# First two blocks' triangular inverses by quarters instead of halves, weight loads on another queue, and VectorE's order fixed around the first chain

## The chip, the cores and the metric

One core of one Trainium2 chip. The metric is the device time of one execution in microseconds; the median of three runs is compared. PE is the matmul engine (PEld its weight loads), DVE is VectorE, ACT is ScalarE, POOL is GpSimd, SP is SyncE, which here only issues DMAs.

## The reference

Linear attention with the delta rule, then a two-layer network on its output:

```python
for t in range(S):                       # B=4, H=8, S=768, D=48
    y[:, :, t] = einsum('bhd,bhde->bhe', q[t], state)
    v_old = einsum('bhde,bhd->bhe', state, kt)          # kt: normalized key
    state = state + bt * einsum('bhd,bhe->bhde', kt, vt - v_old)
...
x = attn_out as (3072, 384)
h = x @ w_in                              # w_in 384 x 2048
out = maximum(0.01 * h, h) @ w_out        # w_out 2048 x 384
```

## The kernel before

The 768 steps are cut into 12 blocks of C = 64. In a block, the 32 heads (8 heads of 4 sequences) are independent; they lie in two groups `g` of 16. For each block `n` these stages run:

- `gram(n)`: PE forms, for each head, keys times keys and keys times queries (`pg`). ACT copies the first part to `gs`, which goes out to DRAM (`gd`) and comes back as `L` with one half of one head a partition. DVE masks the second part into `rq`, one ring buffer `q` a group.
- `inv(b)`: DVE computes norms and coefficients (`norms`), scales L and inverts the unit triangular 32x32 halves of each head's 64x64 matrix by elimination (`eliminate`: one step a column, two products and two subtractions). The first call handles blocks 0 and 1 together (`NB[0] = [0, 1]`, all 128 partitions), later calls one block each. The result T goes out to DRAM, also transposed by ACT (`Tt`).
- `merge(n, g, t)`: the halves come back by DMA, into `t` and `gm`; two products on PE (`pz`, `pu`) with copies by ACT and DVE (`zs`, `rt`) give the block that joins the halves.
- `solve(n)`: per group loads of k, v and q (`rk`, `rv`, `rq`), then `pk`, `pw`, `pc` (state) and `py` (output) on PE with ACT copies between them. `rv` is multiplied by the norms on DVE.
- `columns(n)`: PE transposes y; `split` makes a high and a low part of it (`xh` by ACT, `xl` by DVE).
- `ffn(n)`: 16 steps `f`, each nine products to `ph`, the activation by ACT (`gh`), its low part by DVE (`gl`), and six products to `po`.

The two weight matrices come as 32 tiles `w_all[:, k // 2, k % 2]` of 128x384 64-bit words (a double each). `weights()` unpacks tile k into a high and a low float with ACT's `Abs` (L146), seven DVE instructions (L148, L154 to L158, L161) and an ACT cast (L160). `load_w` issues the load, 8 tiles ahead (`WAHEAD`) from tile 14 on; a small DVE memset (L123) in front of the load holds it back to a given place of DVE's order. Only after tile 2f + 1 is unpacked can step f of `ffn(0)` finish. Tiles 0 to 3 are unpacked during the grams, the rest after the first inverse.

The order on each engine is not that of the code: a planner lays all instructions out at build time by priority (order of the trace) and by its own estimate of when inputs are ready. Each engine then runs its list in that order and waits where an input is late. `weave` only sets the order of the trace; `behind(name)` adds the one condition that an instruction comes after the marked one on its engine. DMAs are issued in order from SP's or ACT's queue.

Of the kernel before, what the change touches and what calls it, by code (L numbers as in the profile page):

```python
# [47 lines left out]
def delta_moe_kernel(ctx: ExitStack, tc, kqT, kv, qT, beta, cst, w_all, out, nblk):  # L48
# [31 lines left out]


# [32 lines left out]
    def split(src, hi, lo):  # L114
        nc.scalar.copy(hi, src)
        nc.vector.tensor_tensor(lo, src, hi.bitcast(F32), ALU.subtract)  # L116
# [10 lines left out]
    def weights():  # L127

        for k in range(2 * NFC):
            f, x = k // 2, k % 2
            words = raws.pop(k).bitcast(F32).rearrange("p (n two) -> p two n", two=2)
            lo, hi = words[:, 0], words[:, 1]
            loi, hii = lo.bitcast(U32), hi.bitcast(U32)
            g = sb.tile([P, DO], F32, tag="cg", name=f"cg{k}", bufs=CB)
# [3 lines left out]
            def final():  # L140
                t = sb.tile([P, 2 * DO], F32R, tag=f"w{k}", name=f"w{k}", bufs=1)
                for e in range(2):
                    (wi, wo)[x][e][f] = t[:, e * DO:(e + 1) * DO]
                return (w[f] for w in (wi, wo)[x])

            nc.scalar.activation(g, hi, AF.Abs)  # L146
            with behind("inverse" if k >= KA else None):
                i = nc.vector.tensor_scalar(g, g, HI_MIN, HI_MAX, ALU.max, ALU.min)  # L148
# [8 lines left out]
            nc.vector.scalar_tensor_tensor(ri, loi, 18, ri, ALU.logical_shift_right, ALU.bitwise_or)  # L157
            nc.vector.tensor_scalar(e.bitcast(U32), gi, 0xFF800000, None, ALU.bitwise_and)  # L158
            d0, d1 = final()
            nc.scalar.copy(d0, g)  # L160
# [14 lines left out]
    def gram(n):  # L175
# [11 lines left out]
        if i == 0:  # L187
            Lh[b0] = sb.tile([P, HC, HC], F32, tag="L", name=f"L{b0}", bufs=2)
        gd = dr.tile([64, HC, HC], F32, tag="gd", name=f"gd{n}")
        for g in range(NGR):  # L190
            kq = kqs[g]
            gs = sb.tile([P, 2, NPAIR, C], F32, tag="gs", name=f"gs{n}_{g}", bufs=2)
            gm[n, g] = m = sb.tile([P, 2, GU, HC], F32, tag="gm", name=f"gm{n}_{g}", bufs=GM_BUFS)
# [12 lines left out]
            for c in range(2):  # L206
                for e in range(2):
                    a = e * HS + g * GH + c * GU
                    (nc.sync, nc.scalar)[e if n < 2 else 0].dma_start(
                        gd[a:a + GU].rearrange("l j i -> j l i"),  # L210
                        gs[c * 64 + e * HC:c * 64 + (e + 1) * HC].rearrange("p b u t -> p (b u) t")[:, :, e * HC:(e + 1) * HC])
            qa = of("q", n, g)
            for b in range(2):
                for c in range(2):
                    r = slice(c * 64, (c + 1) * 64)
                    nc.vector.tensor_tensor(  # L216
                        qa[DN, c, b * NPAIR:(b + 1) * NPAIR], pv[b][r, 1],
                        tri[r].rearrange("p (o t) -> p o t", o=1).broadcast_to([C, NPAIR, C]), ALU.mult)
# [12 lines left out]
    def norms(n, n2):  # L231

        p, w = P, HC
        s, r, c, z = (sb.tile([P, wd], F32, tag=t, name=f"{t}{n}", bufs=b)
                      for t, wd, b in (("sr", HC, 1), ("rc", HC, 1), ("cb", HC, 2), ("sq", C, 2)))
        nrm[n] = z
# [11 lines left out]
        nc.vector.tensor_tensor(c, c, r, ALU.mult)  # L248
        for e in range(2):
# [3 lines left out]
    def eliminate(b, L, j, T, m):  # L253


        w = HC - 1 - j
        parts = []
        for x in range(min(m, 2)):
            t = T[:, x:m:2]
            k = t.shape[1]  # L260
            tv = sb.tile([P, 144], F32, tag=f"tmp{x}", name=f"tmp{b}_{j}_{x}", bufs=1)
# [4 lines left out]
            parts.append((tv, t[:, :, j + 1:]))  # L266
        for tv, t in parts:
# [3 lines left out]

    def inv(b):

        for n in NB[b]:
            need(gg, gram, n)
        two = len(NB[b]) > 1
        M = HC if two else HC // 2
# [6 lines left out]
        if two:  # L284
            nc.vector.tensor_copy(X[:, ::HC + 1], c)
        else:
            for e in range(2):
                r = slice(e * 64, e * 64 + 64)
                nc.vector.tensor_copy(X[r, e:M * HC:HC + 2], c[r, e::2])
# [4 lines left out]
        for j in range(HC - 1):  # L294
            eliminate(b, L, j, T, j + 1 if two else j // 2 + 1)
            if j == HC - 2:
                Tt = sb.tile([P, HC * HC], F32, tag="L", name=f"Tt{b}", bufs=2) if two else X[:, M * HC:]
                Tt = Tt.rearrange("p (i m) -> p i m", m=M)
                nc.scalar.copy(Tt.rearrange("p i m -> p m i"), T)
# [12 lines left out]
    def merge(n, g, t):
# [11 lines left out]
        lo, r1 = slice(R0 + HC, P), slice(0, HC)  # L324
        if len(NB[where[n][0]]) == 1:
            r1 = slice(HC, 2 * HC)
            with behind("h"):
                nc.scalar.copy(gt[r1].rearrange("p l (m e) -> p l e m", e=2),
                               gt[0:HC].rearrange("p l (e m) -> p l e m", e=2))
# [24 lines left out]
    def solve(n):  # L354
# [3 lines left out]
        nc.tensor.matmul(ps[DN, 0:HS], nrm[b][i * 64:i * 64 + 64], eye0[i * 64:i * 64 + 64], start=True, stop=True)  # L358
# [3 lines left out]
        def load(g):  # L362
            merge(n, g, of("t", n, g))
# [71 lines left out]
    def columns(n):  # L435
# [4 lines left out]
        for cc in range(NCC):  # L440
# [5 lines left out]
            parts.append((xh, xl))  # L446

# [60 lines left out]
    NS, NF, NI = NSLOT, NFC + 1, HC + 1  # L508
# [28 lines left out]
def _layout(inputs):  # L537
# [20 lines left out]
    bts = np.stack([np.concatenate([bt[0], bt[1]])] + [np.concatenate([bt[n], bt[n]]) for n in range(2, nblk)])  # L558
# [39 lines left out]
```

## Time and profile before

| | us |
|---|---|
| median of 3 runs | 725.72 (724.77 to 726.75) |
| profiled execution: time, span | 727.48, 725.7 |
| busy PE, DVE, ACT, POOL | 627.9, 499.6, 323.8, 7.4 |
| mean granted clock of PE | 0.973 |

Busy time is a sum over the span; a stage can have another limit than the whole. A row of the profile names the line, the engine and the operation, then output and input by the program's names, the shape, the count, the time and what the engine waited for last. Two DVE instructions can overlap by about a tenth of a microsecond in the records, so the time of a sequence is read from starts, not summed from durations.

### The profile page before, as it was taken

To read this page: it belongs to the slowest core of one execution; us is meant where nothing else is said; L and a number is where in the kernel's file an instruction comes from. 1 tells how busy PE (TensorE), PEld (TensorE's weight loads), DVE (VectorE), ACT (ScalarE), POOL (GpSimd) and SP (SyncE) were. 2 spreads that over 40 slices of the span, in tenths; PEclk is the share of its full clock that TensorE was granted. 3 is DMA by queue.
4 is the path that set the end of the run, shared out by engine and by line. 5 is a ranking of instruction groups with operands and counts; after the bars stand their busy time and mean duration, and the time that the engine had idled before them with its cause. 6 is when DMAs were issued, how large, how long until landed. Compare 5 with 4: busy or idle time off the path is not lost.

```text
span 725.7 us, 20966 instructions
## 1 busy us (share of the span) xinstructions
PE 627.9 (87%) x8296; PEld 581.4 (80%) x8296; DVE 499.6 (69%) x2222; ACT 323.8 (45%) x830; POOL 7.4 (1%) x12
## 2 busy tenths in 40 slices
PE   5200789948997999999999999999999999999996
PEld 4100679838986998998989989989989989999996
DVE  7798999999594765866955956947858659532221
ACT  3112656624444463553454444534634635544432
POOL 4000000000000000000000000000000000000000
PEclk9999999967998999999999999999999999999999
DMA  8495783610306427036045064073171260310000
GB/s 196 94 308 106 196 213 91 162 37 23 46 2 121 102 46 162 17 68 153 3 90 131 4 117 105 7 139 77 30 146 48 46 132 2 63 29 2 1 22 23
DMA packets 130786, 60.91 MB, mean 84 GB/s; under 512 B 115392, under 2 KB 118592, under 8 KB 130688
## 3 DMA queue, kind: packets, MB, share of 16 engines
q1 hardware_dynamic: 117376, 56.81, 34.9%
q10 hardware_dynamic: 13312, 2.76, 2.1%
q8 instruction: 65, 1.06, 0.6%
q14 instruction: 33, 0.27, 0.1%
HBM read 46.96 MB, written 12.58 MB: 82 GB/s over the span
## 4 chain that ended last, share of the span: by engine, by line
PE 61%; DVE 22%; DMA 7%; ACT 4%; issue 3%; SPq 2%; ACTq 1%; DVEq 0%
PE ph L468 25%; PE po L458 22%; DMA tt<-T 3%; PE pk L383 3%; DVE rq L216 3%; PE pw L396 3%; DVE rv L388 3%; DVE T L268 2%; DVE tmp L263 2%; PE pu L342 2%; PE pz L334 2%; SPq L307 2%; DVE cg L155 1%; DVE w L161 1%; DVE cr L157 1%
## 5 line engine op out<-in xcount | busy, mean ns | idle before, releaser
L468 PE MATMUL ph<-xh,w 128*128 128x256 f32 x1152 | 257.3, 296 | 10.0 <-DVE gl L475 6.9
L468 PEld LDWEIGHTS ph<-xh,w 128*128 128x128 f32 x1152 | 195.9, 193 | 21.5 <-DVE gl L475 9.7
L458 PE MATMUL po<-w,gh 128*128 128x384 f32 x768 | 192.0, 347 | 8.7 <-ACT w L160 4.9
L475 DVE TENSOR_TENSOR gl<-ph,gh 128x256 fp32r<-128x256 f32 x192 | 80.6, 423 | 134.4 <-ACT ph L473 123.6
L468 PE MATMUL ph<-xl,w 128*128 128x256 f32 x576 | 166.0, 289 | 1.9 <-DVE xl L116 1.1
L472 ACT ACTIVATE gh<-ph 128x256 fp32r<-128x256 f32 x192 | 73.5, 383 | 173.2 <-PE ph L468 170.8
L458 PEld LDWEIGHTS po<-w,gh 128*128 128x128 f32 x768 | 134.1, 193 | 12.1 <-ACT w L160 5.6
L458 PE MATMUL po<-w,gl 128*128 128x384 f32 x384 | 119.7, 345 | 0.0
L468 PEld LDWEIGHTS ph<-xl,w 128*128 128x128 f32 x576 | 111.3, 193 | 4.3 <-DVE xl L116 4.0
L268 DVE TENSOR_TENSOR T<-T,tmp 128x60 f32<-128x60 f32 (+35 forms) x661 | 112.3, 207 | 1.3
L263 DVE TENSOR_TENSOR tmp<-T,L 128x60 f32<-128x60 f32 (+35 forms) x661 | 112.4, 208 | 0.7
L473 ACT ACTIVATE ph<-ph 128x256 f32<-128x256 f32 x192 | 73.1, 381 | 0.0
L458 PEld LDWEIGHTS po<-w,gl 128*128 128x128 f32 x384 | 68.9, 193 | 0.5
L334 PE MATMUL pz<-rt,gm 32*32 32x32 f32 x768 | 19.9, 197 | 34.8 <-DMA rt<-td 34.8
L201 PE MATMUL pg<-kq 48*64 48x128 f32 x768 | 38.5, 301 | 12.5 <-DMA kq<-in_kqT 7.2
L334 PEld LDWEIGHTS pz<-rt,gm 32*32 32x32 f32 x768 | 16.0, 111 | 37.7 <-DMA rt<-td 35.2
L201 PEld LDWEIGHTS pg<-kq 48*64 48x64 f32 x768 | 30.6, 147 | 19.4 <-DMA kq<-in_kqT 8.0
L216 DVE TENSOR_TENSOR rq<-pg,csb 64x256 f32<-64x256 f32 x96 | 40.6, 423 | 1.7
L280 DVE MEMSET T<- 128x512 f32 (+1 forms) x11 | 5.8, 524 | 39.7 <-DMA tt<-T 30.2
L385 ACT ACTIVATE rt<-pk 48x512 f32<-48x512 f32 x44 | 26.1, 593 | 12.6 <-PE pk L383 11.9
L160 ACT CAST w<-cg 128x384 fp32r<-128x384 f32 x32 | 16.1, 510 | 33.6 <-DVE cr L157 24.5
L398 ACT COPY rv<-pw 64x384 f32<-64x384 f32 x48 | 22.7, 472 | 16.1 <-PE pw L396 15.2
(61 smaller groups left out, 651.4 us busy)
## 6 DMA issues: line engine op xcount, KB each, us to landing
wr<-in_w_all SPq DMA_DIRECT2D x32, 384.0 KB, 5.3
kq<-in_kqT SPq DMA_DIRECT2D x44, 192.0 KB, 3.7
L<-gd SPq DMA_DIRECT2D x22, 256.0 KB, 3.9
rk<-in_kv SPq DMA_DIRECT2D x24, 192.0 KB, 3.4
rv<-in_kv SPq DMA_DIRECT2D x24, 192.0 KB, 4.1
rq<-in_qT SPq DMA_DIRECT2D x24, 192.0 KB, 3.8
out<-ob SPq DMA_DIRECT2D x48, 96.0 KB, 2.7
gd<-gs SPq DMA_DIRECT2D x88, 32.0 KB, 2.8
```

The source lines that it names most:

```text
L201: nc.tensor.matmul(ps[b][c * 64:(c + 1) * 64, p * 128:(p + 1) * 128], kq[r, c ^ b, p, 0], kq[r, c ^ b, p].rearrange("p x t -> p (x t)"), s ...
L216: nc.vector.tensor_tensor(qa[DN, c, b * NPAIR:(b + 1) * NPAIR], pv[b][r, 1], tri[r].rearrange("p (o t) -> p o t", o=1).broadcast_to([C, NP ...
L263: nc.vector.tensor_tensor(tv, t[:, :, j:j + 1].broadcast_to([P, k, w]), L[:, j, j + 1:].rearrange("p (o w) -> p o w", o=1).broadcast_to([P ...
L268: i = nc.vector.tensor_tensor(t, t, tv, ALU.subtract)
L334: nc.tensor.matmul(zv[h * 64:h * 64 + HC, u], gt[lo, l], t[lo, h, u, HC:], start=True, stop=True)
L385: nc.scalar.mul(t[UP, c], pv[c * 64:c * 64 + D], -1.0)
L398: nc.scalar.copy(v[DN, c], pv[c * 64:c * 64 + C])
L458: i = nc.tensor.matmul(po[t][:, :DO], a[:, ts_], w[f], start=(f == 0 and k == 0), stop=(f == NFC - 1 and k == 2))
L468: nc.tensor.matmul(ph, a[f][:, cc * P:(cc + 1) * P], x[cc][e], start=(k == 0), stop=(k == 3 * NCC - 1))
L472: nc.scalar.activation(gh, ph, AF.Prelu, alpha=0.01)
L473: i = nc.scalar.activation(ph, ph, AF.Prelu, alpha=0.01)
L475: i = nc.vector.tensor_tensor(gl, ph, gh.bitcast(F32), ALU.subtract)
```

## The change

1. Blocks 0 and 1 get the diagonal quarters (16x16) inverted instead of the halves: `inv_quarters` has 15 steps on 128 partitions (a head's quarter each), with block 0 and block 1 side by side in the free dimension. `eliminate` takes the parts as a list.
2. `merge_quarters` takes the place of `merge` for these two blocks. The inverted quarters and their transposes go to DRAM (`tq`) and come back as `cps`; ACT spreads them into block-diagonal 64x64 matrices F (`Tt`, `T`) with a mask. Twice, the inverse is doubled by products on PE: z = G times Tt, masked by DVE (`above`), then Tt + (T, z) and T + (z, T), where the addition is a product with the identity into the same accumulation. The second time only Tt is needed and goes to `t`.
3. For these blocks `gs` takes the place of `gm`, two writes of whole rows to `gd` replace four, and L is read in runs of 16 elements. The `gm` copies on DVE go for these two blocks. All inverse and merge DMAs now stand in SP's queue.
4. Weight loads are issued from GpSimd's queue, tiles 4 to 13 behind block 1's last `rq`.
5. The DVE work of weights is held behind marks: 4 to 8 behind the inverse, 9 and 10 behind block 0's first z, 11 to 15 behind its second, 16 on behind the last `xl` of block 0. ACT's `Abs` runs two tiles ahead, its cast one tile late.
6. The constants `cst` grow from 226 to 394 columns; `beta` has another order for blocks 0 and 1.

```diff
     def load_w(k, gate=None):
...
-            with behind("L"):
-                nc.sync.dma_start(raw, w_all[:, k // 2, k % 2])
+            nc.gpsimd.dma_start(raw, w_all[:, k // 2, k % 2])
...
-            nc.scalar.activation(g, hi, AF.Abs)
-            with behind("inverse" if k >= KA else None):
+            with behind(next((GATES[i] for i in sorted(GATES, reverse=True) if k >= i), None)):
                 i = nc.vector.tensor_scalar(g, g, HI_MIN, HI_MAX, ALU.max, ALU.min)
...
+            if k >= LAG:
+                d, s = firsts.pop(0)
+                nc.scalar.copy(d[:, :DO], s)
...
+    def inv_quarters():
...
+        for j in range(HQ - 1):
+            eliminate(0, [(L[:, n], T[:, n, 0:j + 1]) for n in range(2)], j, HQ - 1 - j)
+            if j == HQ - 2:
+                for n in range(2):
+                    nc.scalar.copy(Tt[:, n].rearrange("p i m -> p m i"), T[:, n])
+                    tq = dr.tile([2, P, HQ, HQ], F32, tag="tq", name=f"tq{n}", bufs=2)
+                    for k, x in enumerate((T, Tt)):
+                        nc.sync.dma_start(tq[k].rearrange("p m i -> p (m i)"), x[:, n].rearrange("p m i -> p (m i)"))
...
+    def merge_quarters(n, g, t):
...
+        if g == 0:
+            cps[n] = cp = sb.tile([P, 2, 2 * GU, HQ], F32, tag="gs", name=f"tc{n}", bufs=2)
+            for k in range(2):
+                for c in range(2):
+                    nc.sync.dma_start(
+                        cp[c * 64:(c + 1) * 64, k],
+                        tq[k, c * 64:(c + 1) * 64].rearrange("(x q) m i -> (q m) x i", q=4))
+        F = sb.tile([P, 2, GU, C], F32, tag="kq", name=f"tf{n}_{g}", bufs=KQ_BUFS)
+        for q in range(4):
+            nc.scalar.mul(F[:, :, :, q * HQ:(q + 1) * HQ], cps[n][:, :, g * GU:(g + 1) * GU], quart[:, q:q + 1])
+        Tt, T = F[:, 0], F[:, 1]
...
+        for i in range(2):
+            pz = products(f"pz{i}_", G, Tt)
+            z = sb.tile([P, GU, C], F32, tag="yt", name=f"tz{n}_{g}_{i}", bufs=YT_BUFS)
+            d = nc.vector.tensor_tensor(z, pz, above[i].rearrange("p (o t) -> p o t", o=1).broadcast_to([P, GU, C]), ALU.mult)
...
+            pt = products(f"pu{i}_", T, z, Tt)
+            if i == 0:
+                pv = products(f"pv{i}_", z, T, T)
+                nc.scalar.copy(Tt, pt)
+                nc.scalar.copy(T, pv)
...
+        for c in range(2):
+            nc.scalar.copy(t[DN, c], pt[c * 64:(c + 1) * 64])
...
-    weave(1, (iv, NI, 0, 1))
-    weave(1, (sv, NS, 0, 1))
+    weave(1, (iv, HQ + 1, 0, 1))
     for k in range(KA, WEARLY):
-        load_w(k)
+        load_w(k, "rq")
+    weave(NS + 2 * NM, (sv, NS + 2 * NM, 0, NS + 2 * NM), (wg, NS + 2 * NM, 0, NS + 2 * NM))
...
-CB = 3
+GATES = {4: "inverse", 9: "z0", 11: "z1", 16: "xl"}
+CB, AHEAD, LAG = 4, 2, 1
```

`products` makes one 64x64 product for each of the 16 heads of a group (two, accumulated, where there is an addition):

```python
    def products(name, l, r, add=None):
        p = ps_a.tile([P, 512], F32, tag="a", name=f"{name}{n}_{g}")
        for u in range(GU):
            for c in range(2):
                h = slice(c * 64, (c + 1) * 64)
                o = p[h, u * C:(u + 1) * C]
                if add is not None:
                    nc.tensor.matmul(o, eye[h, h], add[h, u], start=True, stop=False)
                nc.tensor.matmul(o, l[h, u], r[h, u], start=add is None, stop=True)
        return p.rearrange("p (u t) -> p u t", u=GU)
```

More of the change, by code (lines that the diff above doesn't have):

```diff
@@ L78, in delta_moe_kernel @@
     half = csb[:, C + P + HS:C + P + HS + 2]
+    x0 = C + P + HS + 2
+    eye1, quart0, quart = csb[:, x0:x0 + HS], csb[:, x0 + HS:x0 + HS + 4], csb[:, x0 + HS + 4:x0 + HS + 8]
+    above = [csb[:, x0 + HS + 8 + i * C:x0 + HS + 8 + (i + 1) * C] for i in range(2)]
     NR = dict(k=KT_BUFS, q=Q_BUFS, t=KT_BUFS, v=2 * NGR)
@@ L231, in norms @@
     def norms(n, n2):
[L233 to L236, printed above, removed]
+        s, r, c = (sb.tile([P, HC], F32, tag=t, name=f"{t}{n}", bufs=b)
+                   for t, b in (("sr", 1), ("rc", 1), ("cb", 2)))
         dq(2 * n).dma_start(c, beta[n])
@@ L251, in norms, with eliminate @@
         return c
[L253 to L259, printed above, removed]
+    def eliminate(b, parts, j, w):
+        tvs = []
+        for x, (L, t) in enumerate(parts):
             k = t.shape[1]
-            tv = sb.tile([P, 144], F32, tag=f"tmp{x}", name=f"tmp{b}_{j}_{x}", bufs=1)
+            tv = sb.tile([P, 96], F32, tag=f"tmp{x}", name=f"tmp{b}_{j}_{x}", bufs=1)
             tv = tv[:, 0:k * w].rearrange("p (x w) -> p x w", x=k)
@@ L270, in eliminate @@
             mark["inverse"] = i.ins
-    def inv(b):
[L274 to L277, printed above, removed]
+    def inv_quarters():
+        for n in range(2):
+            need(gg, gram, n)
+        X = sb.tile([P, HC * HC], F32, tag="T", name="T0", bufs=1)
+        T, Tt = (X[:, i * 512:(i + 1) * 512].rearrange("p (n m i) -> p n m i", n=2, m=HQ) for i in range(2))
+        nc.vector.memset(T, 0.0)
+        yield
+        L = Lh.pop(0)
+        c = norms(0, L.rearrange("p n m i -> p n (m i)")[:, :, ::HQ + 1])
+        c2 = c.rearrange("p (n i) -> p n i", n=2)
+        nc.vector.tensor_copy(T.rearrange("p n m i -> p n (m i)")[:, :, ::HQ + 1], c2)
+        for n in range(2):
+            nc.vector.tensor_tensor(L[:, n], L[:, n], c2[:, n:n + 1].broadcast_to([P, HQ, HQ]), ALU.mult)
+        yield
+        for j in range(HQ - 1):
+            eliminate(0, [(L[:, n], T[:, n, 0:j + 1]) for n in range(2)], j, HQ - 1 - j)
+            if j == HQ - 2:
+                for n in range(2):
+                    nc.scalar.copy(Tt[:, n].rearrange("p i m -> p m i"), T[:, n])
+                    tq = dr.tile([2, P, HQ, HQ], F32, tag="tq", name=f"tq{n}", bufs=2)
+                    for k, x in enumerate((T, Tt)):
+                        nc.sync.dma_start(tq[k].rearrange("p m i -> p (m i)"), x[:, n].rearrange("p m i -> p (m i)"))
+                    Tts[n] = tq
+                done.add((inv, 0))
+            yield
+    def inv(b):
+        if b == 0:
+            yield from inv_quarters()
+            return
+        n = NB[b][0]
+        need(gg, gram, n)
+        M = HC // 2
         X = sb.tile([P, HC * HC], F32, tag="T", name=f"T{b}", bufs=1)
@@ L283, in inv @@
         c = norms(b, L.rearrange("p m i -> p (m i)")[:, ::HC + 1])
[L284 to L289, printed above, removed]
+        for e in range(2):
+            r = slice(e * 64, e * 64 + 64)
+            nc.vector.tensor_copy(X[r, e:M * HC:HC + 2], c[r, e::2])
         for x in range(2):
@@ L323, in merge @@
         zs = sb.tile([P, 2, GU, HC], F32, tag="yt", name=f"zs{n}_{g}", bufs=YT_BUFS)
[L324 to L329, printed above, removed]
+        lo = slice(R0 + HC, P)
+        r1 = slice(HC, 2 * HC)
+        with behind("h"):
+            nc.scalar.copy(gt[r1].rearrange("p l (m e) -> p l e m", e=2),
+                           gt[0:HC].rearrange("p l (e m) -> p l e m", e=2))
         with behind("po"):
@@ L420, in solve @@
             stages.pop(3)
+        if n < 2:
+            for _ in zip_longest(*(merge_quarters(n, g, of("t", n, g)) for g in range(NGR))):
+                yield
         for s in range(NSLOT):
```

150 lines of the change are left out of this document (108 added, 42 removed).

## The prediction

> **What bounds the kernel now.** I read first the table of busy time by stage; its cuts follow the waits and the order of time.
>
> ```profile
> 0.00:33.50 33.50, 13.14 (x128) 11.20 (x128) 25.22 (x57) 8.00 (x17) 7.35 (x12) 1.00 0.59 138
> 33.50:40.20 6.70, 0.42 (x2) 0.28 (x2) 6.18 (x20) 0.71 (x3) 0.00 (x0) 1.00 1.02 247
> 40.20:62.30 22.10, 0.00 (x0) 0.00 (x0) 22.10 (x131) 1.65 (x3) 0.00 (x0) 1.00 0.72 217
> 62.30:70.30 8.00, 0.00 (x1) 0.00 (x1) 6.64 (x17) 2.02 (x1) 0.00 (x0) 1.00 0.92 173
> 70.30:96.60 26.30, 19.47 (x372) 17.23 (x372) 24.33 (x78) 17.82 (x40) 0.00 (x0) 0.94 0.77 194
> 96.60:172.70 76.10, 61.58 (x730) 54.28 (x730) 73.47 (x254) 38.06 (x96) 0.00 (x0) 0.84 0.43 104
> 172.70:250.00 77.30, 71.36 (x893) 65.94 (x892) 52.78 (x279) 34.34 (x90) 0.00 (x0) 0.93 0.35 69
> 250.00:700.00 450.00, 441.72 (x6038) 412.61 (x6037) 285.06 (x1384) 214.35 (x562) 0.00 (x0) 1.00 0.32 66
> ```
>
> The columns are the stretch, its length, then busy time of PE, PEld, DVE, ACT and POOL, the granted clock, the DMA share and GB/s. From 250 us on PE is the bound (441.7 of 450). Up to 172.7 it is DVE: 22.1 of 22.1 us in the first pair's elimination, 73.5 of 76.1 us while ffn(0) waits for unpacked weights. So what counts is when DVE is through with the weights; PE then follows from block 1 on. The order of time gives the milestones:
>
> ```profile
> 33.55 0.19 DVE L239 TENSOR_SCALAR sr<-L 128x32 uint32<-128x32 uint32 x1 [4.17 <-DMA L<-gd]
> 40.18 0.29 DVE L263 TENSOR_TENSOR tmp<-T,L 128x31 f32<-128x31 f32 x2
> 60.68 0.62 DVE L148 TENSOR_SCALAR cg<-cg 128x384 f32<-128x384 f32 x2
> 62.33 2.02 ACT L299 COPY Tt<-T 128x1024 f32<-128x1024 f32 x1 [19.52 <-DVE T L268]
> 70.30 1.06 PE L334 MATMUL pz<-rt,gm 32*32 32x32 f32 x32 [33.37 <-DMA rt<-td]
> 77.63 3.91 PE L396 MATMUL pw<-rv,rt 128*64 128x48 f32 x63
> 96.16 0.42 DVE L116 TENSOR_TENSOR xl<-px,xh 128x256 fp32r<-128x256 f32 x1
> ```
>
> Here L arrives (33.55), the inverse ends (62.3), its DRAM round trip ends (70.3), `pw` starts (77.6), and the last `xl` of block 0 ends (96.6). From L to the end of the inverse: 28.8 us. From there to the last `xl`: 34.3 us. After that the rest of the weights: 76.1 us.
>
> **The change, part by part.** DVE prices first.
>
> ```profile
> 41.32 0.28 DVE L263 TENSOR_TENSOR tmp<-T,L 128x30 f32<-128x30 f32 x2
> 41.77 0.35 DVE L263 TENSOR_TENSOR tmp<-T,L 128x58 f32<-128x58 f32 x2
> 42.29 0.33 DVE L263 TENSOR_TENSOR tmp<-T,L 128x56 f32<-128x56 f32 x2
> 36.86 1.28 DVE L292 TENSOR_TENSOR L<-L,cb 128x512 f32<-128x512 f32 x2
> 38.17 1.97 DVE L388 TENSOR_TENSOR rv<-rv,nt 64x384 f32<-64x384 f32 x4
> 86.27 0.35 DVE L148 TENSOR_SCALAR cg<-cg 128x384 f32<-128x384 f32 x1
> 88.76 0.35 DVE L148 TENSOR_SCALAR cg<-cg 128x384 f32<-128x384 f32 x1
> L216 DVE TENSOR_TENSOR rq<-pg,csb 64x256 f32<-64x256 f32 x32 | 13.5, 423 | 0.7
> L388 DVE TENSOR_TENSOR rv<-rv,nt 64x384 f32<-64x384 f32 x12 | 5.9, 555 | 0.1
> L346 DVE TENSOR_SCALAR rt<-pu 32x256 f32<-32x256 f32 x4 | 1.7, 422 | 0.1
> L336 DVE COPY zs<-pz 32x256 f32<-32x256 f32 x4 | 1.7, 413 | 0.0
> ```
>
> Elimination. A step of four instructions takes 0.45 us at 30 elements (41.32 to 41.77) and 0.52 at 58 (41.77 to 42.29). The new one has 15 steps of 15 to 64 elements: 15 x 0.50 = 7.5 us (6.8 to 8.0), where 31 steps took 20 (40.18 to 60.68, less two weight instructions). Scaling L goes from 1.28 to some 0.7 us, and two small products for `nrm` add about 0.3. The norms and the four `rv` products (1.97 us) stay. From L to the end of the inverse I get 6.6 - 0.3 + 7.5 = 13.8 us, against 28.8: **15.0 us earlier**. Clearing a smaller T and the eight dropped `gm` copies lie ahead of 33.5 us, where DVE idled 33.5 - 25.2 = 8.3 us; they count as nothing.
>
> The doublings. Each z is one DVE product of 128x512. Between 256 and 384 elements (423, 555 ns) the slope is 1.03 ns an element, so 0.69 us; eight are 5.5 us, half of them for block 1. The four `zs` and four `rt` instructions of blocks 0 and 1 go: 3.3 us. PE and ACT prices:
>
> ```profile
> 253.41 1.99 PE L383 MATMUL pk<-rt,rk 64*48 64x64 f32 x64
> L385 ACT ACTIVATE rt<-pk 48x512 f32<-48x512 f32 x44 | 26.1, 593 | 12.6 <-PE pk L383 11.9
> L205 ACT COPY gs<-pg 128x256 f32<-128x256 f32 x48 | 15.9, 375 | 29.8 <-PE pg L201 29.8
> L299 ACT COPY T<-T 128x512 f32<-128x512 f32 x10 | 10.7, 1068 | 0.0
> ACT w L160 <- DVE cr L157: 7.7, 9, 1.4
> td<-T ACTq DMA_DIRECT2D x4, 128.0 KB, 3.9
> rt<-td ACTq DMA_DIRECT2D x8, 64.0 KB, 2.5
> ```
>
> A 64x64 product is two PE instructions of 31 ns (64 in 1.99). A group (n, g) needs 16 + 32 + 32 + 16 + 32 = 128 products, 7.9 us of PE; for block 0 they are on the path, for block 1 (15.9 us) they lie beside ffn(0), where PE was busy 61.6 of 76.1 us at a clock of 0.84. That cover is nearly used up, not gone.
>
> Block 0's path from the end of the inverse:
> - Transposing copy: half of 1068 ns, 0.5 us; writing: 3.9 us; reading: four DMAs in a row, 64 B pieces where there were 128 B ones. Bounds 2.5 us (a 64 KB read) and 2 x 3.9. I take 5.4, nearer the 128 KB row since bytes and pieces match it. Sum 9.8 (the old round trip: 8.0).
> - F, four ACT products of 256 elements at 375 ns: 1.3; first product 1.0; z 0.7; the second group comes 1.2 later. z0 at 14.0.
> - Products 0 of both groups fill PE for 7.9 us from 12.8; second product 1.0; z1 0.7. z1 at 22.4.
> - Last products 2.0; two copies to `t` at 593 ns, 1.2. `pw` at 25.6, against 15.3 before (77.6 - 62.3).
> - `pw` to the last `xl`: 19.0 us before. Some of it was ACT holding `rv`, `ys` and `xh` copies behind weight casts that waited for DVE (7.7 us in nine waits); the new code casts one weight late and takes absolute values two ahead. Bounds 11.3 (all of that gone) and 19.0; I take 14.5, as not all nine lie here.
>
> That makes 40.1 us against 34.3: **5.8 later**. DVE has for it weights 4 to 15 (12 x 2.49 us, from 86.27 and 88.76, = 29.9), four z (2.8) and three `xl` (1.3): 34.0. So the gates cost about 6 us of idle DVE, most of it between z0 and z1, where only weights 9 and 10 are given, and just ahead of `xl`. Before, it idled 8.0 - 6.64 + 26.3 - 24.33 = 3.3 us there.
>
> After the last `xl` the same 16 weights remain. Before, weight 16 was half done there (1.2 us more to do now), and block 1's `zs` and `rt` go (1.7 less). Block 1's z (2.8) fall behind `xl` or into the idle 6 us: between -0.5 and 2.3 on the 76.1 us. I take **+1.5**, since block 1's products stand behind block 0's in PE's order.
>
> Loads and queues. 32 weight loads leave SP's queue for GpSimd's; loads 0 to 3 now stand behind eight memsets, loads 4 to 13 behind block 1's last `rq`. Two `gd` writes a group go instead of four, and L is read in 64 B pieces.
>
> ```profile
> 3.44 4.44 POOL L98 MEMSET rq<- 64x1024 f32 x4
> 21.58 3.98 PE L201 MATMUL pg<-kq 48*64 48x128 f32 x32 [5.22 <-issue]
> kq<-in_kqT SPq DMA_DIRECT2D x44, 192.0 KB, 3.7
> kq<-in_kqT SPq DMA_DIRECT2D x4, 192.0 KB, 8.1
> L102 DVE COPY rk<-csb 64x768 f32<-64x768 f32 x2 | 2.6, 1328 | 0.3 <-DMA csb<-in_cst 0.3
> ```
>
> The first weights come some 6 us later (POOL is busy until 7.9 us). That leaves DVE free for `rq` at first, and the last gram, for which PE idled 5.2 us, may start earlier; but the constants are larger and L's pieces smaller. Bounds -5.2 and +3; I take **-1.0**, nearer zero, since 8.3 us of slack on DVE cuts both ways. No DMA issued from GpSimd is in this trace, so its issue is bounded by zero (loads run weights ahead) and by the second case below. SP, ahead of L, the quarters and the inputs, loses work; counted as nothing.
>
> The row of `L102` (1328 ns for 768 elements, beside POOL's memsets) shows DVE and POOL holding each other up. The Trainium skill, in SBUF — State Buffer, section "SBUF: two separate sides", says that a DMA issued from GpSimd has its descriptors written by GpSimd and waits while VectorE is in a two-port instruction; it gives 3.1 us for one of 0.62. By that figure 16 loads in 76 us still keep pace, so the time would stay; no run here shows it.
>
> The sum: -15.0 + 5.8 + 1.5 - 1.0 = **-8.7 us**. The profiled execution took 727.5 us (span 725.7), so 718.8; it stood 1.8 above the median of 725.7, and against that I forecast **717 us**.
>
> **The rivals.**
> 1. Shorter chain and earlier grams: `pw` to `xl` at 11.3 and the gram's 5.2 us won: -3.2 and -4.2 more, some 709.5. For it: the nine ACT waits. Against: it needs both.
> 2. Nothing won between `pw` and `xl` (19.0): 4.5 us later, 721.5. For it: more ACT work (eight F products and the doublings' copies) in the same queue.
> 3. Slower: the round trips run into the weight backlog. DMA was full (1.02, then 0.72 of 22.1 us) until about 56; the inverse now ends near 46, and GpSimd's loads start ahead of L's last read. A 192 KB load took 3.7 us in the median and 8.1 in the backlog, 4.4 more. Three legs (L, writing T, reading it) make 13.2 us: 730. It decides from 8.7 / 3 = 2.9 us a leg. Against: loads that began at 34 now begin near 29, and gram 2's inputs come later, so the backlog ends sooner.
> 4. GpSimd starves DVE of weights: 16 weights in 76.1 us is one in 4.8; at 5.4 each, 10 us are lost: 727. The rule of the Trainium skill (SBUF — State Buffer) named above leads here only at a worse figure than its own.
>
> **How the numbers follow.** The forecast (712 to 721 by its own terms) has 0.50, rival 1 0.12, rival 2 0.13, rival 3 0.15, rival 4 0.05; 0.05 is left, 0.03 of it near 725. Faster by over 0.3% (2.2 us, about what these runs can tell from no change) is the first three, 0.75; within it 0.08; slower 0.17. The range 706 to 728 reaches over rivals 1, 2 and 4, and leaves out rival 3 and a tail.
>
> **What would show it.** Right: elimination of block 0 near 7.5 us; inverse to last `xl` near 40; DVE idle 4 to 8 us between them; ffn(0)'s weights done near 164; PE full from there. Wrong: `pz` of the quarters over 14 us behind the inverse (rival 3), the first instruction of a weight waiting for its load (rival 4), or PE, not DVE, full in ffn(0), with block 1's 15.9 us of products in front of it.

## The result, and the profile after

The changed kernel takes 742.65 us (741.12 to 746.52, four executions) against 725.5 before: ratio 1.0243, 95% interval 1.0201 to 1.0284, so 17.6 us slower. The forecast was 717 (706 to 728). The profiled execution took 742.7 us with a span of 740.9 at a mean granted clock of 0.975, near the 0.973 of before; 740.9 - 725.7 = 15.2 us are there to be explained. Ratios leave out single executions in a slower state, such as the profiled one of e1 (928 us at a granted clock of 0.672).

The busy time by stage, cut at the last `xl` of block 0 and at the last weight instruction of DVE (columns as in the prediction):

```profile
0.00:108.00 108.00, 43.13 (x854) 39.65 (x854) 73.18 (x245) 39.32 (x85) 20.50 (x36) 0.95 0.58 152
108.00:158.60 50.60, 35.46 (x639) 32.17 (x639) 49.90 (x142) 23.83 (x52) 4.40 (x8) 0.82 0.41 111
158.60:740.90 582.30, 567.38 (x7573) 530.42 (x7573) 367.03 (x1779) 272.20 (x717) 0.00 (x0) 0.99 0.32 67
```

The last `xl` comes at 108.0, not at 96.6. DVE is nevertheless through with the weights at 158.6, 14 us earlier than before (172.7), 50.6 us behind that `xl` where it took 76.1. The weights did not get cheaper: 16 of them at the 2.49 us of the prediction are 39.8 us, before and after. What went is other work of DVE. It ran 254 instructions in that stage before and 142 now; block 2's elimination, 8 of the 16 masks `rq` and 11 of the 15 `gl` are not among them, because PE delivered what they need later (block 2's L is in use at 162.6, before at 111.8). And still the time is longer: in those 50.6 us PE was busy for 35.5 only.

The path to that `xl`, from the order of time on DVE and ACT (start, duration, engine and line, what it waited for):

```profile
44.07 0.19 DVE L280 TENSOR_SCALAR sr<-L 128x32 uint32<-128x32 uint32 x1 [10.91 <-DMA L<-gd]
57.78 0.30 DVE L316 TENSOR_TENSOR T<-T,tmp 128x15 f32<-128x15 f32 x2
68.01 3.30 ACT L398 ACTIVATE tf<-tc,csb 128x256 f32<-128x256 f32 x8 [4.99 <-DMA tc<-tq]
74.39 0.68 DVE L416 TENSOR_TENSOR tz<-pz,csb 128x512 f32<-128x512 f32 x1
83.95 0.69 DVE L416 TENSOR_TENSOR tz<-pz,csb 128x512 f32<-128x512 f32 x1 [0.24 <-PE pz L409]
87.34 0.51 ACT L183 CAST w<-cg 128x384 fp32r<-128x384 f32 x1 [4.67 <-DVE cg L171]
89.65 1.18 ACT L427 COPY rt<-pu 64x512 f32<-64x512 f32 x2
90.86 1.71 ACT L398 ACTIVATE tf<-tc,csb 128x256 f32<-128x256 f32 x4
94.56 1.18 ACT L427 COPY rt<-pu 64x512 f32<-64x512 f32 x2
107.21 0.76 DVE L125 TENSOR_TENSOR xl<-px,xh 128x256 fp32r<-128x256 f32 x2 [1.38 <-ACT xh L124]
```

L is used at 44.07 (before 33.55), and DVE idled 10.91 us for it. The inverse ends at 57.78 + 0.30 = 58.08. Behind z1 (84.64) the copies to `t`, which release `pw`, come at 89.65 and 94.56: ACT stood 4.67 us at a weight cast that waited for DVE, and built `F` for block 1 in between. (The x2 rows are the two copies of one group, so the first group's `t` is complete at 90.83 and the second's at 95.74.)

Why L came late, by the chain of waits (first row), the rows of POOL's and SP's queues, and the issues between 15 and 60 us:

```profile
29.57 14.40 DMA L<-gd
...
28.05 4.22 POOL L135 DMA_DIRECT2D wr<-in_w_all  x8 [17.96 <-DVE wr L134]
...
30.01 7.83 SPq L487 DMA_DIRECT2D rk<-in_kv  x1
...
L<-gd SPq DMA_DIRECT2D x2, 128.0 KB, 8.6
```

The second read of L is issued at 29.57 and lands 14.40 us later. From 28.05 to 32.27, eight weight loads of 384 KB went out from GpSimd's queue, 0.53 us each: some three ahead of L's read and the others right behind it.

What stood in front of ffn(0), by the `gl` rows on DVE (one for each step f, counted from 0). First the twelfth row of the kernel before, then three of the changed kernel:

```profile
139.88 0.42 DVE L475 TENSOR_TENSOR gl<-ph,gh 128x256 fp32r<-128x256 f32 x1
...
115.84 0.42 DVE L600 TENSOR_TENSOR gl<-ph,gh 128x256 fp32r<-128x256 f32 x1
146.40 0.44 DVE L600 TENSOR_TENSOR gl<-ph,gh 128x256 fp32r<-128x256 f32 x1
158.58 0.76 DVE L600 TENSOR_TENSOR gl<-ph,gh 128x256 fp32r<-128x256 f32 x2
```

The row of step 1 stands at 115.84 and that of step 2 at 146.40, so three steps have come by 147 us; in the kernel before there were twelve. In PE's order nearly all of block 1's products and block 2's grams stand between the two, with waits of 3.7 us for a copy by ACT, 1.9 for block 1's z on DVE and 3.0 for ACT's copies to `t` (`rt`). So the weights were there and PE was not.

### The profile page after: what moved, and what is told of

Read it like the earlier page. It is cut to its first block, busy times and chain, and to the rows that moved or that the text cites. A ratio compares the mean times of both kernels' runs of the same rounds, so it can differ in the third digit from the quotient of the medians.

```text
span 740.9 us, 22480 instructions
## 1 busy us (share of the span) xinstructions
PE 646.0 (87%) x9064; PEld 602.2 (81%) x9064; DVE 490.1 (66%) x2164; ACT 335.4 (45%) x853; POOL 24.9 (3%) x44
## 4 chain that ended last, share of the span: by engine, by line
PE 67%; DVE 17%; DMA 6%; ACT 4%; issue 3%; SPq 2%; POOL 1%; ACTq 0%; DVEq 0%; POOLq 0%
PE ph L593 26%; PE po L583 23%; PE pw L517 3%; PE pk L504 3%; DVE rv L509 3%; DMA tt<-T 2%; DVE rq L254 2%; PE py L535 2%; DMA L<-gd 2%; PE pu L459 2%; PE px L567 2%; DVE cg L171 1%; PE pz L451 1%; PE pc L525 1%; DVE T L316 1%
## 5 line engine op out<-in xcount | busy, mean ns | idle before, releaser
L583 PE MATMUL po<-w,gh 128*128 128x384 f32 x768 | 189.3, 342 | 6.2 <-ACT gh L597 6.2
L583 PEld LDWEIGHTS po<-w,gh 128*128 128x128 f32 x768 | 131.6, 190 | 8.7 <-ACT gh L597 8.4
L316 DVE TENSOR_TENSOR T<-T,tmp 128x31 f32<-128x31 f32 (+8 forms) x630 | 104.6, 204 | 1.3
L311 DVE TENSOR_TENSOR tmp<-T,L 128x31 f32<-128x31 f32 (+8 forms) x630 | 104.9, 204 | 0.7
L235 PE MATMUL pg<-kq 48*64 48x128 f32 x768 | 35.3, 306 | 15.7 <-DMA kq<-in_kqT 8.3
L235 PEld LDWEIGHTS pg<-kq 48*64 48x64 f32 x768 | 28.3, 150 | 22.3 <-DMA kq<-in_kqT 8.4
L517 PEld LDWEIGHTS pw<-rv,rt 128*64 128x64 f32 x768 | 24.7, 141 | 9.5 <-issue 6.0
L517 PE MATMUL pw<-rv,rt 128*64 128x48 f32 x768 | 26.6, 227 | 6.3 <-issue 5.8
L409 PE MATMUL pz<-tf,gm 64*64 64x64 f32 x256 | 10.3, 242 | 23.5 <-ACT tf L398 22.4
```

The costliest lines, as they stand in the source:

```text
L235: nc.tensor.matmul(ps[b][c * 64:(c + 1) * 64, p * 128:(p + 1) * 128], kq[r, c ^ b, p, 0], kq[r, c ^ b, p].rearrange("p x t -> p (x t)"), s ...
L311: nc.vector.tensor_tensor(tv, t[:, :, j:j + 1].broadcast_to([P, k, w]), L[:, j, j + 1:].rearrange("p (o w) -> p o w", o=1).broadcast_to([P ...
L316: i = nc.vector.tensor_tensor(t, t, tv, ALU.subtract)
L517: nc.tensor.matmul(pv[r, u], t[:, c, u], v[:, c, u], start=True, stop=True)
L583: i = nc.tensor.matmul(po[t][:, :DO], a[:, ts_], w[f], start=(f == 0 and k == 0), stop=(f == NFC - 1 and k == 2))
```

## The experiments

Three theories. **A**: the loads from GpSimd, in flight beside L's read, cost their 10.5 us. **B**: PE's order, with block 1's doublings and block 2's grams ahead of most of ffn(0), gives away what DVE wins. **C**: PE's added work, some 16 to 18 us, is a flat price. Later a fourth: weights woven into block 0's chain stretch it. Ratios are to the kernel before, run again beside each set of experiments (medians 725.8 to 727.8 us), and differences in us are differences of ratios times 725.7; the interval of one ratio is 0.2 to 0.4% to either side.

**e1, the loads kept on GpSimd but issued behind L.**

```diff
-        load_w(k, "rq")
+        load_w(k, "norm0")      # the first DVE instruction that reads L
```

> The changed kernel, with tiles 4 to 13 held behind the first DVE instruction that reads L (it was block 1's last rq). Theory A (the weights in flight when L is read delay it: 14.4 us instead of 3.6, and DVE starts the inverse 10.5 us late): L lands about 33, and the time falls by about 10, to 732. Rival B (what keeps the time up is PE's order: block 1's doublings and gram 2 ahead of ffn(0) from 113 to 159 us; L's lateness is absorbed there): L lands about 33 all the same, but the time stays within 3 of 742.

Ratio 1.0152 (1.0112 to 1.0192), 6.6 us less than the change, between A's 10 and B's 3. The early rows are taken from the trace of e4 (below), which issues the loads in the same place; its transfers are those between 25 and 62 us:

```profile
wr<-in_w_all POOLq DMA_DIRECT2D x13, 384.0 KB, 11.1
tq<-T SPq DMA_DIRECT2D x4, 128.0 KB, 2.9
...
L<-gd SPq DMA_DIRECT2D x1, 128.0 KB, 2.9
...
40.23 0.36 DVE L172 TENSOR_SCALAR cr<-wr 128x384 uint32<-128x384 uint32 x1 [4.33 <-DMA wr<-in_w_all]
```

L's read falls to 2.9 us and L is in use at 32.56, 11.5 us earlier. But now a weight instruction that the planner put ahead of the elimination waits 4.33 us for its load, and the next round trip still meets the loads: writing T takes 2.9 us (1.8 in the changed kernel), and z0 ends 17.0 us behind the inverse, as in the changed kernel (14.4 in e2, without loads from GpSimd). Holding the loads back by one leg does not take them out of the way of the next.

**e2, the loads back on SP's queue, behind L.**

```diff
-            nc.gpsimd.dma_start(raw, w_all[:, k // 2, k % 2])
+            with behind("L"):
+                nc.sync.dma_start(raw, w_all[:, k // 2, k % 2])
```

> The changed kernel with the weight loads back in SP's queue behind the reads of L, as before; all else changed. Theory A: about 732, like the first, since the cause is that the loads run beside L's read, from whichever queue. Rival (GpSimd's queue itself is slow or starved): clearly below the first kernel, 725 or less, with weights waiting less. Rival B: within 3 of 742.

Ratio 1.0079 (1.0043 to 1.0115): 11.9 us of the 17.6 come back. L and the stage after the last `xl`:

```profile
32.27 0.19 DVE L281 TENSOR_SCALAR sr<-L 128x32 uint32<-128x32 uint32 x1 [5.39 <-DMA L<-gd]
...
97.30:148.00 50.70, 34.64 (x639) 31.47 (x638) 50.00 (x141) 23.85 (x52) 0.00 (x0) 0.82 0.41 109
```

L is used at 32.27, 11.8 us earlier, and the last `xl` ends at 97.3, 10.7 earlier. Behind it nothing changed: PE is busy for 34.6 of 50.7 us (35.5 of 50.6 in the changed kernel), and 631.9 us remain to the end (632.9). Ten weight loads follow L's read here too, 0.4 us behind it, and the read takes 3.4 us: behind it in one queue they hardly slow it. So the harm came with the separate queue, or with the loads issued ahead of the read; that loads are under way is not enough. A holds for the first part, and only for that.

**e3, the kernel before with GpSimd's loads alone.**

```diff
 # in the kernel before
-            with behind("L"):
-                nc.sync.dma_start(raw, w_all[:, k // 2, k % 2])
+            nc.gpsimd.dma_start(raw, w_all[:, k // 2, k % 2])
...
-        load_w(k)
+        load_w(k, "rq")
```

> The kernel before with one part of the change alone: weight loads from GpSimd's queue, tiles 4 to 13 behind block 1's last rq; halves, merge and gates as before. Theory A: L's last read (4 KB runs here, 3.6 us before) is late too, though less if large pieces share the DMA engines better than 64 B pieces: between 3 and 10 us slower than 725.5. Rival (64 B pieces alone are slow, the queue is harmless): L lands within 1 us of before, and the time is 725 to 727.

Ratio 1.0056 (1.0031 to 1.0082), 4.1 us slower. The loads cost here too, but not at L, as A had it: L's read takes 3.8 us in the median, as before. The norms begin at 37.31 (33.55 before), and a weight instruction stood in front of them that waited 4.09 us for its load, which took 9.05 us to land. The loads went out 1.6 us behind L's last read here (30.29 and 28.66), and that read consists of 4 KB pieces, so e3 doesn't tell the size of L's pieces from the order of issue.

**e4, e1 with another order.** Block 1's ten doubling steps are traced among ffn(0)'s steps, and its F tiles take L's buffers, so that block 2's keys need not wait for them.

```diff
-        F = sb.tile([P, 2, GU, C], F32, tag="kq", name=f"tf{n}_{g}", bufs=KQ_BUFS)
+        F = sb.tile([P, 2, GU, C], F32, tag="kq" if n == 0 else "L", name=f"tf{n}_{g}", bufs=2)
...
-    weave(NS + 2 * NM, (sv, NS + 2 * NM, 0, NS + 2 * NM), (wg, NS + 2 * NM, 0, NS + 2 * NM))
+    weave(NS + NM, (sv, NS + NM, 0, NS + NM), (wg, NS + 2 * NM, 0, NS + NM))
...
-(sv, NS * (n + 1 < nblk), 2, 11)
+(sv, NS * (n + 1 < nblk) + NM * (n == 0), 2, 11)
```

> The first kernel, and block 1's doublings traced among ffn(0)'s steps instead of ahead of them, with F of block 1 in the two buffers of L instead of those of kq, so that gram 2's inputs needn't wait for it. The arithmetic and the instructions are the same. Theory B: PE stood still for 15 us between 116 and 159 us, and ffn(0) passed from 2 to 3 steps there; in the new order the idle goes: about 15 below the first kernel, 717. Rival C (the added PE work, 18 us busy, is a flat price in any order): within 4 of the first kernel.

Ratio 1.0022 (1.0002 to 1.0042), 9.4 us less than e1, where B had asked for 15. From the last `xl` (101.0) to the end it takes 625.7 us.

**e5, the order alone.** The changed kernel with e4's order; loads as changed.

> The changed kernel with its loads left on GpSimd's queue and where they were, and only the order changed: block 1's ten doubling steps traced among ffn(0)'s steps, not ahead of them, and its two T tiles in the buffers that L had, so that block 2's grams need not wait for them. If PE's order is a large part of the 17 us (theory B), some 8 to 10 us come back without touching the loads: 732 to 735. If the loads in front of L are all that counts (theory A), nothing comes back: 741 to 744. If 18 us of added PE work is a flat price (theory C), 741 to 744 as well.

Ratio 1.0070 (1.0045 to 1.0095), 12.6 us less than the change, somewhat more than B asked for. The last `xl` ends at 104.7 (3.3 earlier), 625.4 us remain (632.9). L was in use 2.2 us earlier (41.87), which the edit doesn't explain. Behind the `xl`, where the order acts, it is worth 7.5 us here, and 7.9 on top of e2 (631.9 to 624.0 in e6).

**e6, loads on SP and the order.** e2's and e4's edits together.

> The changed kernel with its loads back on SP's queue behind L's read, and block 1's doublings among ffn(0)'s steps with their tiles in L's buffers. Loads alone gave 731.8 (e2), order on gated loads gave 10.4 us (738.9 to 728.5). If A and B add up, 731.8 - 10.4 = 721 (718 to 725), under the kernel before. If both give the same time back once, so that after the one the other brings nothing, 728 to 732. Under theory C, where PE has 18 us more to do whatever the order, no order gets below the kernel before, 726.

723.07 us (the kernel before 727.76 beside it), ratio 0.9942 (0.9920 to 0.9964): **4.2 us faster than the kernel before**. Stages, cut as for the changed kernel, and `gl` on DVE:

```profile
97.20:149.20 52.00, 44.45 (x775) 40.88 (x775) 50.48 (x149) 25.01 (x59) 0.00 (x0) 0.93 0.36 95
149.20:721.20 572.00, 554.05 (x7438) 516.86 (x7437) 362.87 (x1764) 269.38 (x710) 0.00 (x0) 1.00 0.32 67
...
114.03 0.42 DVE L601 TENSOR_TENSOR gl<-ph,gh 128x256 fp32r<-128x256 f32 x1
130.40 0.42 DVE L601 TENSOR_TENSOR gl<-ph,gh 128x256 fp32r<-128x256 f32 x1
147.72 0.42 DVE L601 TENSOR_TENSOR gl<-ph,gh 128x256 fp32r<-128x256 f32 x1
```

DVE needs the same 50 us or so for the rest of the weights, but PE is busy for 44.5 of 52 at a clock of 0.93, in place of 0.82. Nine steps of ffn(0) have come by 148 us; in the changed kernel it was three by 147. From the last `xl` 624.0 us remain. A and B are two separate costs: 11.9 and 12.6 us alone, 21.8 together. That no order gets below the kernel before, as C had it, is refuted.

**e7, e6 without the gates at z0, z1 and xl.**

```diff
-GATES = {4: "inverse", 9: "z0", 11: "z1", 16: "xl"}
+GATES = {4: "inverse"}
```

> As e6, with the gates on weights 9, 11 and 16 taken away (those at z0, z1 and xl), so that VectorE may take any weight after the end of block 0's inverse. If the gates hold back work that PE's first steps need later (DVE idle ahead of xl in the trace of the changed kernel), 2 to 5 us less than e6. If the gates do what they say, keeping weight work out of the chain's way, the doublings wait for DVE and it is 2 to 5 us more than e6.

Ratio 1.0144 (1.0118 to 1.0169), 14.7 us slower than e6, far beyond the 2 to 5 expected. DVE's order:

```profile
64.73 0.69 DVE L417 TENSOR_TENSOR tz<-pz,csb 128x512 f32<-128x512 f32 x1
89.59 0.71 DVE L417 TENSOR_TENSOR tz<-pz,csb 128x512 f32<-128x512 f32 x1
...
119.84 0.45 DVE L125 TENSOR_TENSOR xl<-px,xh 128x256 fp32r<-128x256 f32 x1
```

Between z0 and z1 DVE unpacks weights for 24 us with one wait of 2.2, while the chain stands. The last `xl` ends at 120.3, 23.1 later than in e6, and only 7.1 us of that come back behind it. So the shorter elimination needs the gates: without the three of them it is lost altogether.

**e8, e6 without block 1's doublings.**

```diff
+        if n == 1:
+            yield
+            for c in range(2):
+                nc.scalar.copy(t[DN, c], Tt[c * 64:(c + 1) * 64])
+            yield
+            return
```

> As e6, with block 1's doublings left out (its T is used as the quarters left it, so the output is not the reference's): PE has 10 us less to do (the pz, pu and pv of block 1), DVE and ACT some 8 us less between them. Theory C: the time falls by PE's whole 10 us, since PE is full from there to the end. Theory B: block 1's doublings fit into holes of PE in ffn(0) once the order allows it, and the time falls by 0 to 4 us.

785.84 us, ratio 1.0799 (1.0767 to 1.0831): less work, 62 us more. It doesn't answer its question, since the planner laid PE's order out anew, and block 2's merge came ahead of its own data. PE's longest wait between 98 and 220 us is

```profile
PE pz L458 <- DMA rt<-td: 14.8, 1, 14.8
```

This is a part of the 62 us; the rest no run took apart.

**e12, e6 with block 1's products issued twice**, which leaves the order as it is (the rows of `gl`, z and the copies come in e6's sequence) and asks the same the other way round.

```diff
+            if n == 1 and not name.startswith("d"):
+                products("d" + name, l, r, add)
             return p.rearrange("p (u t) -> p u t", u=GU)
```

> e6 with each of block 1's product groups issued twice, the second time into a PSUM tile that nothing reads, in the same place of PE's order: 512 more PE instructions of 31 ns, 15.9 us, and no more work for VectorE or ScalarE. If PE's work is a flat price wherever it stands (theory C), the time grows by 14 to 17 us, to some 739. If block 1's products lie beside ffn(0) in holes that PE has there anyway (PE idles 9 us from 100 to 175 in e6), it grows by 0 to 7 us. In between (7 to 14) both are partly so.

744.7 us, ratio 1.0253 (1.0220 to 1.0286): 22.6 us over e6, or 17.4 by the two spans (738.6 and 721.2; the profiled execution of e12 is its fastest). Stages of e12 with e6's cuts:

```profile
97.20:149.20 52.00, 42.74 (x956) 39.84 (x957) 48.08 (x131) 21.32 (x48) 0.00 (x0) 0.93 0.29 81
149.20:738.60 589.40, 570.06 (x7766) 532.74 (x7762) 365.54 (x1775) 273.18 (x717) 0.00 (x0) 0.99 0.32 66
```

In the 52 us, PE does 181 more instructions and is busy no longer (42.7 against 44.5): block 1's products push ffn(0)'s work out of the stage, and all of it comes at the end (589.4 for 572.0). The 7.5 us that PE idles there in e6 took none of it. Over the whole span PE is busy 13.7 us longer (658.0 for 644.3) and idle 3.7 longer; 9.2 us of its waits stand at doubled products, for ACT's copies, since the doubles take PSUM tiles of the same ring of four. So what goes beyond PE's own time may be the experiment's. On this point C is right: PE work added in this place costs its full time.

**e9, block 0's chain by itself.**

```diff
-GATES = {4: "inverse", 9: "z0", 11: "z1", 16: "xl"}
+GATES = {4: "xl"}
```

> e6 with every weight from 4 on gated behind the last xl of block 0, so that block 0's chain has VectorE and ScalarE to itself; the weights are done after it, and the time gets longer by some 25 us (12 weights of 2.5 us that lay beside the chain, less what VectorE idled there). What counts is the chain. If the forecast's steps were right (round trip 9.8, z0 at 14.0, z1 at 22.4, pw at 25.6, last xl at 40.1 or less behind the inverse) and the weights woven in cost the rest, the last xl ends 36 to 41 us behind the inverse, against 48.0 in e6. If the steps themselves were sized too small, it stays at 45 to 48.

Ratio 1.0204 (1.0163 to 1.0245), 19.0 us over e6 where 25 were expected. The edit put the weights elsewhere than meant: the mark `xl` does not exist yet when those ahead of it are traced, so these weights ran among the steps of the elimination, which ends at 77.64 here, and not behind the chain. From ACT's copy of T on, the chain stands alone:

```profile
77.91 1.08 ACT L340 COPY T<-T 128x256 f32<-128x256 f32 x2
84.86 6.49 ACT L399 ACTIVATE tf<-tc,csb 128x256 f32<-128x256 f32 x16 [4.51 <-DMA tc<-tq]
...
90.34 0.69 DVE L417 TENSOR_TENSOR tz<-pz,csb 128x512 f32<-128x512 f32 x1 [1.01 <-PE pz L410]
100.58 0.69 DVE L417 TENSOR_TENSOR tz<-pz,csb 128x512 f32<-128x512 f32 x1 [0.24 <-PE pz L410]
...
104.38 1.18 ACT L428 COPY rt<-pu 64x512 f32<-64x512 f32 x2 [0.69 <-PE pu L410]
...
113.75 0.76 DVE L125 TENSOR_TENSOR xl<-px,xh 128x256 fp32r<-128x256 f32 x2 [2.22 <-ACT xh L124]
```

From the copy to the end of the last `xl` (114.51): 36.6 us. In e6 it is 48.0 from the end of the inverse. The steps' own lengths were about right. Of the 11.4 us between the two, 1.6 stand ahead of z0, 0.1 between z0 and z1, and 6.4 between z1 and the second group's `t`, where ACT waits for casts in e6 (4.14 us at once) and the granted clock is 0.75, in e9 1.00. The last 3.3 stand between that `t` and the last `xl`; the rows of this stretch, e6's and then e9's (columns as in the prediction):

```profile
84.94:97.17 12.23, 11.91 (x178) 10.61 (x178) 6.43 (x16) 9.01 (x21) 0.00 (x0) 0.66 0.36 102
105.56:114.51 8.95, 8.87 (x194) 8.03 (x194) 1.18 (x4) 5.94 (x14) 0.00 (x0) 1.00 0.55 137
```

PE shows busy nearly throughout in both, at a granted clock of 0.66 in e6 and 1.00 in e9. So these 3.3 us go with the lower clock rather than with a wait; what lowered it no run took apart.

**e10, e6 with `AHEAD` and `LAG` at 0.**

```diff
-CB, AHEAD, LAG = 4, 2, 1
+CB, AHEAD, LAG = 4, 0, 0
```

> e6 with the absolute values no longer taken two weights ahead and the cast no longer one weight late, as in the kernel before. If that part of the change keeps ScalarE's copies from standing behind casts, taking it away puts the last xl 3 to 5 us later and the time 3 to 5 us up (726 to 728). If it only moves the wait (in e6 a cast and an absolute value still hold ScalarE for 4.1 and 1.2 us after z1, ahead of the copies to t), the time stays within 2 us of e6's.

Ratio 0.9972 (0.9950 to 0.9994), 2.2 us over e6, and the intervals overlap. The last `xl` ends at 98.0 (97.2). So that part brings some 2 us, not clear of the noise.

**e11, e6 with block 0's copies to `t` on DVE.**

```diff
-            nc.scalar.copy(t[DN, c], pt[c * 64:(c + 1) * 64])
+            d = (nc.vector.tensor_copy if n == 0 else nc.scalar.copy)(t[DN, c], pt[c * 64:(c + 1) * 64])
+        if n == 0:
+            mark["z1"] = d.ins
```

> e6 with block 0's four copies to t on VectorE in place of ScalarE, and weights 11 to 15 given after them in place of after z1. In e6 the copies start 5.0 and 9.6 us after the end of z1 (79.19 and 83.76 against 74.20), though PE needs 4 us for the products between, because ScalarE stands at a cast and an absolute value that wait for VectorE. If that wait is what the forecast's pw at 25.6 lacked, pw's second group starts 4 to 5 us earlier and the time falls by 2 to 5 us (ratio to the kernel before 0.987 to 0.991). If the weights held back then come back behind xl, VectorE loses as much as the chain wins and the time is that of e6.

722.12 us, ratio 0.9938 (0.9918 to 0.9957): the lowest of all, but the same as e6 within the interval. First e6's order around the copies, then e11's:

```profile
32.33 0.19 DVE L281 TENSOR_SCALAR sr<-L 128x32 uint32<-128x32 uint32 x1 [5.65 <-DMA L<-gd]
48.85 0.30 DVE L317 TENSOR_TENSOR T<-T,tmp 128x15 f32<-128x15 f32 x2
63.15 0.69 DVE L417 TENSOR_TENSOR tz<-pz,csb 128x512 f32<-128x512 f32 x1
73.51 0.69 DVE L417 TENSOR_TENSOR tz<-pz,csb 128x512 f32<-128x512 f32 x1 [1.26 <-PE pz L410]
76.89 0.51 ACT L184 CAST w<-cg 128x384 fp32r<-128x384 f32 x1 [4.14 <-DVE cg L172]
79.19 1.18 ACT L428 COPY rt<-pu 64x512 f32<-64x512 f32 x2
83.76 1.18 ACT L428 COPY rt<-pu 64x512 f32<-64x512 f32 x2
96.41 0.76 DVE L125 TENSOR_TENSOR xl<-px,xh 128x256 fp32r<-128x256 f32 x2 [1.48 <-ACT xh L124]
```

```profile
80.03 1.07 PE L520 MATMUL pw<-rv,rt 128*64 128x48 f32 x29 [0.33 <-DVE rt L428]
82.79 0.51 ACT L184 CAST w<-cg 128x384 fp32r<-128x384 f32 x1 [2.18 <-DVE cg L172]
86.47 0.51 ACT L184 CAST w<-cg 128x384 fp32r<-128x384 f32 x1 [0.88 <-DVE cr L174]
89.10 0.47 ACT L540 COPY ys<-py 128x384 f32<-128x384 f32 x1
95.83 0.75 DVE L125 TENSOR_TENSOR xl<-px,xh 128x256 fp32r<-128x256 f32 x2
```

`pw`'s second group starts at 80.03 in place of 84.44, as expected. But then ACT's next copies stand behind the next casts that wait for DVE (2.18, 0.88), and the last `xl` ends at 96.6, against 97.2. The wait moved down the queue.

## Why the prediction was wrong

The stages in us, worked out from the rows shown (e9 from ACT's copy of T, the others from the end of the inverse; the measured z0 and z1 are the second group's). The forecast counts both groups at z0 and one from z1 to `pw`:

| | before | forecast | after | e6 | e9 |
|---|---|---|---|---|---|
| L in use | 33.55 | 32.55 | 44.07 | 32.33 | |
| L to end of inverse | 28.8 | 13.8 | 14.0 | 16.8 | |
| to z0 | | 14.0 | 17.0 | 14.7 | 13.1 |
| to z1 | | 22.4 | 26.6 | 25.1 | 23.4 |
| to the first group's `t` (`pw` can start) | | 25.6 | 32.8 | 31.2 | 25.8 |
| to the second group's `t` | | | 37.7 | 35.8 | 27.7 |
| to the last `xl` | 34.3 | 40.1 | 49.9 | 48.0 | 36.6 |
| from there to the end | 629.1 | 630.6 | 632.9 | 624.0 | 624.1 |

Against before the changed kernel's terms are +10.5, -14.8, +15.6 and +3.8, together 15.1 of the 15.2 us. Against the forecast they are off by +11.5, +0.2, +9.8 and +2.3, together 23.8 us.

**Right.** The elimination: 14.0 us from L to its end, 13.8 forecast. That it came so close is in part luck: where L is there early, the same stage takes 16.8 us (e6). The chain's steps, when it stands alone: z0, z1 and the first `t` within 1.0 us of the forecast, and the last `xl` even 3.5 earlier than the 40.1 (e9). (A slip in the sum: four F products at 375 ns are 1.5 us, not 1.3. Measured are 3.30 for the eight of two groups.)

**Wrong, the loads.** "I take -1.0 ... SP, ahead of L, the quarters and the inputs, loses work; counted as nothing." It was +10.5. I had the collision as rival 3, "the round trips run into the weight backlog", at 4.4 us a leg and a chance of 0.15, and it decided on one leg alone: L's read took 14.40 us. The round trip behind the inverse was 3.0 us longer than forecast as well (z0 at 17.0). The 8.1 us that I took as the price of a backlog was that of 192 KB in large pieces. L's read is 64 B pieces, and eight loads of 384 KB went out around it from another queue. Before, SP's one queue had kept L in front: with the loads issued there behind L again it takes no longer than before (e2). Whether larger pieces would have come through beside the loads no run tried. The Trainium skill says in DMA: Bandwidth & Descriptors, section "Queues, rings and completion order", that a DMA engine takes turns between queues packet by packet. By that, I infer, a read of small pieces gets a small share beside loads of large pieces; the 14.40 us beside the loads, and the 2.9 without them (e4), agree, but the turns themselves no run here shows.

**Wrong, z1 to `pw`.** Forecast 3.2 us for one group; measured 6.2 to the first group's `t` and 11.1 to the second's. I expected that `AHEAD` and `LAG` would keep ACT's copies from standing behind casts, and took 14.5 for `pw` to `xl` on that account. They are worth some 2 us, not clear of the noise (e10). ACT still stood at casts that waited for DVE (4.67 us at once), while DVE took the first instructions of several weights together behind the gate at z1, and F of block 1 stood in the same queue. Taking the copies to `t` off ACT moved the wait to the next copies (e11). Between the inverse and the last `xl` DVE idled 13.9 us, where I had 4 to 8. What remains is that the chain with weights woven in takes 11.4 us more than alone (48.0 against 36.6), of which I had counted nothing: 6.4 lie behind z1, where ACT waits for casts, 3.3 go with PE's lower clock, and 1.6 stand ahead of z0.

**Wrong, the cover of block 1's products.** "For block 1 (15.9 us) they lie beside ffn(0) ... That cover is nearly used up, not gone." It was gone: the products a second time cost 17 to 23 us (e12). I read the 14.5 us that PE idled from 96.6 to 172.7 as room, but PE idled there for weights, and the change gave the last of them 25 us sooner behind the `xl` (50.6 in place of 76.1 us). I had carried the 76.1 us over as if they were the price of the weights alone; about half is other work that DVE does only as PE delivers. So this term had two sides, neither of which I had: DVE through with the weights sooner, and PE with more to do ahead of ffn(0). In the changed kernel they cancel to +3.8; with block 1's work among ffn(0)'s steps the same weights are worth 5.1 us (624.0 against 629.1). My own sign for it ("PE, not DVE, full in ffn(0), with block 1's 15.9 us of products in front of it") came half true: the products stood in front, and PE, waiting for their copies, was not even full.

**Rival 4**, GpSimd's descriptors starved by DVE, did not come. The loads took a median 5.3 us from GpSimd's queue and 5.3 from SP's (e6), and DVE waited for one once, 3.2 us, just ahead of its longer wait for L. The Trainium skill's rule (SBUF — State Buffer, section "SBUF: two separate sides") that such a DMA waits while VectorE is in a two-port instruction left no trace in these medians; what cost time was that the loads came too soon.

**Open.** What PE work costs if it is taken away, as e8 failed to show. What lowered PE's granted clock between `t` and the last `xl` (0.70 in the changed kernel, 0.66 in e6, 1.00 in e9). Whether the size of L's pieces matters beside the loads. Whether the gates alone, in the kernel before, would gain: not tried. And e6's inverse takes 16.8 us, 2.8 longer than the changed kernel's; two waits for `rv`'s load and two weight instructions fall into it, which no run took apart.

## What to carry to other kernels

A load moved to another queue is no longer behind what stood ahead of it in the old one: ask which transfer it will meet, and if it is gated, which comes next and who then waits for the load. An engine's idle time is no room for new work when it is idle for the very thing that the change delivers sooner; count what is late next, and where the new work stands in the order. And a chain over several engines is priced with what stands between its steps on every one of them: a gate on one engine doesn't clear another's queue.

## What the runs showed of the hardware

A read of 128 KB in 64 B pieces took 2.9 us with no weight load issued ahead of it (e4), 3.4 with ten loads of 384 KB issued right behind it in the same queue (e2), and 14.40 with eight such loads from GpSimd's queue around it (the changed kernel). SP's next issue there, of a 192 KB load, then took 7.83 us itself; what held it no run took apart. Issuing eight loads took GpSimd's queue 4.22 us. And 512 more products on PE, which take 31 ns each where they stand in a row, made PE busy 13.7 us longer and the span 17.4 us longer, with no more instructions on any other engine.
